# Where GpSimd waits for the two output DMAs in the closing barrier of a one-token decode kernel

## The chip, the cores and the metric

The kernel runs on one core of one Trainium2 chip. The metric is device time in microseconds (us) of one execution, read over several executions. The profile's *span* runs from the first to the last recorded instruction; in the profiled executions of before the time is 1.79 us more than the span (383.49 against 381.698). All times inside a profile count from the start of the span.

Engines: PE is TensorE, DVE is VectorE, ACT is ScalarE, POOL is GpSimd, SP is SyncE. A name with a small q (POOLq) is that engine's sequencer, under which the profile lists waits, drains and semaphore instructions.

## The reference

It is one decode step, with one token: grouped-query attention over a cache of 65,536 keys with 32 query heads and 4 key/value heads, plus a gated MLP branch, mixed by a sigmoid gate. Cut to what matters:

```python
x = A_x                                             # (1, 1, 1024) bf16
g = sigmoid((x * gate_w).sum(-1, keepdims=True))
a = A_ref(x, k_cache, v_cache, wq, wo)              # k_cache, v_cache: (1, 4, 65536, 128) bf16
b = B_ref(x, w_in, w_sp, b_sp, w_out)
return g * a + (1 - g) * b                          # (1, 1, 1024) bf16
```

Nearly all of the work is reading the two caches and the weights. The result is 2 KB.

## The kernel before

The body loads 162 MB through one ring of buffers, computes along, and ends with the output projection, a cast on ACT and two output DMAs of 1 KB. One is issued by ACT, one by SP:

```python
out_sb = const.tile([P, NO], BF16, name="out_sb")
out_rows = out.rearrange("o t (q n) -> (o t q) n", n=NO)
nc.scalar.copy(out=out_sb[:], in_=out_ps[:])
for i, queue in enumerate((nc.scalar, nc.sync)):
    p0 = (2 * i + 1) * B - 1
    ins = queue.dma_start(out=out_rows[2 * i:2 * i + 2, :], in_=out_sb[p0:p0 + 2, :])
    out_queues.append(ins.ins.name)
```

After the body stands a closing block. Its job is to make sure that every engine and every DMA is done, to reset the semaphores, and to let all engines go. This kernel already rewrites that block into one barrier, in which GpSimd is the hub. The framework gives GpSimd eight instructions there: `l[0]` drain, `l[1]` gather, `l[2]` (dropped), `l[3]` drain, `l[4]` range clear of the semaphores, `l[5]` drain, `l[6]` (dropped), `l[7]` release. The waits for all DMAs and engines, which the framework gives to SP, are hung on `l[0]`:

```python
def close_with_one_barrier(n):
    block = n.main_func.blocks[-1]
    # ... (collects each engine's instructions of the block as l = [(index, kind, ins), ...])
        if engine == mybir.EngineType.Pool:
            # ... (asserts the eight kinds)
            drop += [l[2][0], l[6][0]]
            closer = l[0][0]
            continue
        # ... (SP: takes over the waits; other engines: drop the second barrier)
    final = set()                       # the semaphores of the two output DMAs
    for b in n.main_func.blocks:
        for ins in b.instructions:
            if ins.name in out_queues:
                final |= {u.id for u in ins.sync_info.on_update}
    assert len(final) == len(out_queues)
    waits.sort(key=lambda w: w.id in final)
    block.instructions[closer] = copy.replace(
        block.instructions[closer], sync_info=mybir.SyncInfo(on_wait=waits, on_update=[]))
    for i in sorted(drop, reverse=True):
        del block.instructions[i]
```

There are eleven waits. The build puts wait instructions of two semaphores each in front of it and leaves the last wait on the drain. The semaphores that matter here: S[102] is the ACT output DMA, S[103] the SP output DMA, S[96] the gather (each other engine adds one with its closing drain; in the trace of before S[96] changes 0.001 to 0.013 us after the end of each of these four drains), S[97] the release, S[99] GpSimd's own work. S[105] and S[107] are DVE's and ACT's work.

Of the kernel before, what the change touches and what calls it, by code (L numbers as in the profile page):

```python
# [28 lines left out]
def kernel(  # L29
# [89 lines left out]
    def close_with_one_barrier(n):  # L119
        block = n.main_func.blocks[-1]  # L120
        by = {}
        for i, ins in enumerate(block.instructions):
            by.setdefault(ins.engine, []).append((i, type(ins).__name__, ins))
        drop = []
        waits = None
        for engine, l in by.items():
            kinds = [k for _, k, _ in l]
            if engine == mybir.EngineType.Pool:
                assert kinds == ["InstDrain", "InstEventSemaphore", "InstEventSemaphore",
                                 "InstDrain", "InstISA", "InstDrain", "InstEventSemaphore",  # L130
                                 "InstEventSemaphore"]
                drop += [l[2][0], l[6][0]]
                closer = l[0][0]
                continue
            if engine == mybir.EngineType.SP:
                assert l[0][2].has_wait() and not l[0][2].has_update()
                waits = list(l[0][2].sync_info.on_wait)
                drop.append(l[0][0])
                l, kinds = l[1:], kinds[1:]
            assert kinds == ["InstDrain", "InstEventSemaphore"] * 2  # L140
            drop += [l[1][0], l[2][0]]
        final = set()
        for b in n.main_func.blocks:
            for ins in b.instructions:
                if ins.name in out_queues:
                    final |= {u.id for u in ins.sync_info.on_update}
        assert len(final) == len(out_queues)
        waits.sort(key=lambda w: w.id in final)
        block.instructions[closer] = copy.replace(
            block.instructions[closer], sync_info=mybir.SyncInfo(on_wait=waits, on_update=[]))  # L150
        for i in sorted(drop, reverse=True):
            del block.instructions[i]

    nc.at_finalize(close_with_one_barrier)

    kv = big.tile([P, NKV * CT * P], BF16, name="kv")
# [405 lines left out]
```

## Time and profile before

| | before |
|---|---|
| median of 3 runs | 383.50 us (383.31 to 383.65) |
| span of the profiled run | 381.698 us |
| DMA engines busy | 9 tenths in 39 of 40 slices, 425 GB/s mean |
| two output DMAs issued | 379.721 us (SP), 379.725 us (ACT) |
| their semaphores complete | 380.853 us (ACT), 381.028 us (SP) |
| last arrival to the end of the span | 0.670 us |

The page of the kernel before: total span, the DMA rows of its 40 equal slices, and the chain of work that ended last, by engine and then by line:

```profile
span 381.7 us, 2586 instructions
...
DMA  9999999999999999999999999999999999999995
GB/s 376 438 419 422 433 435 440 433 471 415 407 426 440 440 441 426 440 433 440 440 428 440 440 440 433 434 427 426 412 433 441 433 440 413 428 419 433 433 414 220
...
## 4 chain that ended last, share of the span: by engine, by line
DMA 60%; PE 20%; DVE 15%; issue 1%; ACT 1%; SPq 1%; DVEq 0%; ACTq 0%
```

The chain in order of time has as its last long piece the load of A_wo (start in us, length in us, what):

```profile
347.56 31.38 DMA kv<-in_A_wo_dram
```

The kernel is bound by its loads, and this one ends at 378.94 us. A change to its last 2 us can't move the total by more than half a per cent. Here is the end of the timeline of the kernel before (start in us, length in us, engine, line, operation, operands, and in brackets the idle time before it and what ended it):

```profile
378.98 0.29 PE L475 MATMUL out_ps<-kv,oa 128*32 128x256 bf16 x4 [0.36 <-DMA kv<-in_A_wo_dram]
379.32 0.37 ACT L518 CAST out_sb<-out_ps 128x256 bf16<-128x256 f32 x1 [45.57 <-PE out_ps L475]
379.72 0.32 SPq L521 DMA_DIRECT2D out_dram<-out_sb  x1
379.73 0.25 ACTq L521 DMA_DIRECT2D out_dram<-out_sb  x1
```

After 379.73 us no engine computes any more. What fills the rest are sequencer instructions, which the timeline leaves out, but the view of one source line shows them. All of the close has one line (L557, the end of the kernel's context). Below are its instructions that ran between the issue of the output DMAs and the last arrival at 381.03 us (engine, operation, count, shortest/median/longest duration in ns, first and last start in us):

```profile
L557 ACTq DRAIN  x1: 241/241/241, 380.0 to 380.0; - x1
L557 SPq DRAIN  x1: 177/177/177, 380.1 to 380.1; - x1
L557 POOLq EVENT_SEMAPHORE  x1: 43/43/43, 380.9 to 380.9; - x1
```

And the same view after the last arrival, 381.03 to 381.7 us:

```profile
L557 POOLq EVENT_SEMAPHORE  x3: 17/17/42, 381.1 to 381.6; - x3
L557 POOLq DRAIN  x3: 34/41/72, 381.1 to 381.5; - x3
L557 POOLq EVENT_SEMAPHORE_RANGE_CLEAR  x1: 96/96/96, 381.4 to 381.4; - x1
```

So before the arrival GpSimd does one wait, and after it seven instructions. The exact order is in the single records of the trace. The table gives for each of GpSimd's instructions its start, the start counted from the last arrival, and the *step*, which is the distance to the start of the next one:

```
kernel before        start us   from arrival   step us
wait S[102],S[105]    380.877      -0.151       0.175
   (S[103] complete at 381.028: the last arrival)
wait S[103],S[107]    381.052      +0.024       0.087
drain (waits S[99])   381.139      +0.111       0.085
gather (S[96])        381.224      +0.196       0.080
drain                 381.304      +0.276       0.101
range clear           381.405      +0.377       0.125
drain                 381.530      +0.502       0.064
release (S[97])       381.594      +0.566
end of span           381.698      +0.670
```

The engines had all reported to S[96] by 380.272 us, so the gather had nothing to wait for at 381.224. It only stood behind an instruction that did. The reset and the release show in the trace too: S[99] to S[110] change 0.021 to 0.069 us after the range clear starts, and the other engines' last instructions start 0.041 to 0.053 us after the release does.

### The profile page before, as it was taken

To read this page: it belongs to the slowest core of one execution; us is meant where nothing else is said; L and a number is where in the kernel's file an instruction comes from. 1 tells how busy PE (TensorE), PEld (TensorE's weight loads), DVE (VectorE), ACT (ScalarE), POOL (GpSimd) and SP (SyncE) were. 2 spreads that over 40 slices of the span, in tenths; PEclk is the share of its full clock that TensorE was granted. 3 is DMA by queue.
4 is the path that set the end of the run, shared out by engine and by line. 5 is a ranking of instruction groups with operands and counts; after the bars stand their busy time and mean duration, and the time that the engine had idled before them with its cause. 6 is when DMAs were issued, how large, how long until landed. Compare 5 with 4: busy or idle time off the path is not lost.

```text
span 381.7 us, 2586 instructions
## 1 busy us (share of the span) xinstructions
PE 229.4 (60%) x1372; PEld 56.6 (15%) x796; DVE 218.4 (57%) x211; ACT 39.6 (10%) x55; POOL 4.4 (1%) x10
## 2 busy tenths in 40 slices
PE   0433465678157934796379539762977196749355
PEld 0110011112011200121011101110111011212123
DVE  4241487996689306966996058669860497550040
ACT  1010001111601100114011001140100010500000
POOL 4000000000000000000000000000000000000000
PEclk9996569998669885989598958995889599969768
DMA  9999999999999999999999999999999999999995
GB/s 376 438 419 422 433 435 440 433 471 415 407 426 440 440 441 426 440 433 440 440 428 440 440 440 433 434 427 426 412 433 441 433 440 413 428 419 433 433 414 220
DMA packets 4376, 162.17 MB, mean 425 GB/s; under 512 B 521, under 2 KB 525, under 8 KB 909
## 3 DMA queue, kind: packets, MB, share of 16 engines
q1 hardware_dynamic: 4324, 162.01, 98.7%
q8 instruction: 8, 0.13, 0.1%
q14 instruction: 4, 0.02, 0.0%
q10 hardware_dynamic: 40, 0.01, 0.0%
HBM read 162.01 MB, written 0.00 MB: 424 GB/s over the span
## 4 chain that ended last, share of the span: by engine, by line
DMA 60%; PE 20%; DVE 15%; issue 1%; ACT 1%; SPq 1%; DVEq 0%; ACTq 0%
DMA kv<-in_A_k_cache_dram 38%; PE s_ps L388 15%; DVE kv L381 9%; DMA kv<-in_A_wo_dram 8%; DMA kv<-in_A_wq_dram 7%; DMA kv<-in_A_v_cache_dram 7%; PE o_ps L434 3%; DVE pt L424 2%; DVE mx L383 1%; DVE o_sb L448 1%; PE q_ps L274 1%; ACT sc L421 1%; DVE rowt L444 1%; ACT sc L399 1%; SPq L165 1%
## 5 line engine op out<-in xcount | busy, mean ns | idle before, releaser
L388 PE MATMUL s_ps<-kv,wt 128*128 128x512 bf16 x512 | 138.1, 427 | 85.4 <-DVE kv L381 85.4
L381 DVE STREAM_TRANSPOSE kv<-kv 128x2048 int32<-128x2048 int32 x64 | 142.7, 2280 | 58.8 <-DMA kv<-in_A_k_cache_dram 58.8
L434 PE MATMUL o_ps<-kv,pt 128*64 128x512 bf16 x512 | 62.6, 404 | 7.5 <-DMA kv<-in_A_v_cache_dram 7.5
L388 PEld LDWEIGHTS <-wt 128*128 128x128 bf16 x256 | 27.1, 106 | 197.7 <-issue 133.8
L399 ACT CAST sc<-s_ps 128x1024 bf16<-128x1024 f32 x16 | 16.2, 1013 | 253.0 <-PE s_ps L388 253.0
L434 PEld LDWEIGHTS <-pt 128*64 128x64 bf16 x256 | 16.2, 116 | 51.3 <-issue 48.4
L424 DVE STREAM_TRANSPOSE pt<-sc 128x1024 bf16<-128x1024 bf16 x16 | 18.6, 1217 | 6.8 <-ACT sc L421 6.8
L444 DVE TENSOR_TENSOR rowt<-o_ps,own 128x1024 f32<-128x1024 f32 x4 | 4.8, 1195 | 25.7 <-PE o_ps L434 25.7
L421 ACT ACTIVATE sc<-sc,nb 128x1024 bf16<-128x1024 bf16 x16 | 18.2, 1137 | 12.2 <-DVE nb L417 12.2
L383 DVE TENSOR_REDUCE mx<-sc 128x1 f32<-128x1024 bf16 x12 | 14.5, 1206 | 7.0 <-ACT sc L399 7.0
L454 PE MATMUL om_ps<-o_sb,hsel 128*32 128x128 f32 x8 | 2.5, 421 | 19.7 <-DVE o_sb L448 19.7
L403 DVE TENSOR_REDUCE mx<-sc 128x1 f32<-128x1024 bf16 x4 | 4.9, 1220 | 13.6 <-ACT sc L399 13.6
L274 PE MATMUL q_ps<-kv,xT 128*32 128x512 bf16 x64 | 7.2, 630 | 7.3 <-DMA kv<-in_A_wq_dram 7.3
L274 PE MATMUL z_ps<-kv,xT 128*32 128x448 bf16 x64 | 6.4, 577 | 3.9 <-DMA kv<-in_B_w_in_dram 3.9
L475 PE MATMUL out_ps<-kv,oa 128*32 128x256 bf16 x128 | 6.5, 364 | 3.3 <-DMA kv<-in_A_wo_dram 1.9
L341 DVE TENSOR_TENSOR rowt<-q_ps,own_b 128x512 f32<-128x512 f32 x2 | 1.3, 686 | 12.4 <-PE q_ps L274 12.4
L448 DVE TENSOR_REDUCE o_sb<-rowt 128x128 f32<-128x1024 f32 x4 | 7.5, 1872 | 0.1
L289 DVE TENSOR_TENSOR rowt<-z_ps,own_b 128x448 f32<-128x448 f32 x2 | 1.2, 620 | 8.6 <-PE z_ps L274 8.6
L274 PEld LDWEIGHTS <-xT 128*32 128x32 bf16 x64 | 3.0, 139 | 19.3 <-issue 19.3
L230 PE MATMUL xb_ps<-xg,spread 8*128 8x256 bf16 x1 | 0.4, 367 | 9.0 <-DMA xg<-in_gate_w_dram 9.0
L475 PEld LDWEIGHTS <-oa 128*32 128x32 bf16 x128 | 4.5, 129 | 5.5 <-issue 2.7
L518 ACT CAST out_sb<-out_ps 128x256 bf16<-128x256 f32 x1 | 0.4, 372 | 45.6 <-PE out_ps L475 45.6
(88 smaller groups left out, 54.9 us busy)
## 6 DMA issues: line engine op xcount, KB each, us to landing
kv<-in_A_k_cache_dram SPq DMA_DIRECT2D x4, 4096.0 KB, 26.8
kv<-in_A_wq_dram SPq DMA_DIRECT2D x2, 4096.0 KB, 32.9
kv<-in_A_v_cache_dram SPq DMA_DIRECT2D x2, 4096.0 KB
kv<-in_B_w_in_dram SPq DMA_DIRECT2D x2, 3584.0 KB, 15.1
kv<-in_A_wo_dram SPq DMA_DIRECT2D x1, 4096.0 KB
kv<-in_B_w_out_dram SPq DMA_DIRECT2D x1, 3584.0 KB
kv<-in_A_wo_dram SPq DMA_DIRECT2D x1, 2048.0 KB, 28.1
kv<-in_A_wo_dram SPq DMA_DIRECT2D x1, 1024.0 KB, 30.2
```

Source lines behind the costliest of these rows:

```text
L274: ins = nc.tensor.matmul(ps[t * B:(t + 1) * B, k * HN:k * HN + n], lhsT=xT[:, i * KH + c:i * KH + c + 1].to_broadcast([P, B]), rhs=w[:, c, ...
L381: nc.vector.transpose(out=kb[:, v * n:(v + 1) * n], in_=kb[:, v * n:(v + 1) * n])
L383: nc.vector.reduce_max(**late.pop())
L388: ins = nc.tensor.matmul(s_ps[:, k * HN:(k + 1) * HN], lhsT=wt[g % 2][:, v, b].rearrange("p a v h -> p (a v h)"), rhs=kx[:, b // 2, b % 2, ...
L399: nc.scalar.copy(out=sct[g, j][:], in_=s_ps[:])
L403: nc.vector.reduce_max(**late.pop())
L421: nc.scalar.activation(out=sct[g, j][:], in_=sct[g, j][:], func=ACT.Exp, scale=SCALE, bias=nb[:, 0:1], accum_out=lss[g][:, j:j + 1])
L424: nc.vector.transpose(out=ptt[g, j][:].rearrange("p c x -> p (c x)"), in_=sct[g, j][:])
L434: ins = nc.tensor.matmul(o_ps[g][hs, e, :], lhsT=ptt[g, j][:, 2 * u:2 * u + 2, :].rearrange("p c x -> p (c x)"), rhs=vx[:, 2 * u + e], sta ...
L444: nc.vector.tensor_tensor(out=om8, in0=o_ps[g][:].rearrange("p e (v d) -> p (e v) d", d=DH), in1=own_8[:].unsqueeze(2).to_broadcast([P, 2 ...
L448: nc.vector.tensor_reduce(out=o_sb[:], in_=om8.rearrange("p x d -> p d x"), axis=AX.X, op=ALU.add)
L475: nc.tensor.matmul(out_ps[t * B:(t + 1) * B, :], lhsT=vec[:, c0 + c:c0 + c + 1].to_broadcast([P, B]), rhs=w[:, c, t * NO:(t + 1) * NO], st ...
```

## The change

The intent is to let GpSimd do its first drain and the gather while the output DMAs are still on their way, and to wait for these two DMAs only at the second drain, just before the semaphores are reset. That they must have arrived by then is my argument. What the trace of before shows is that the reset reaches their semaphores: S[102] and S[103] change once more 0.025 and 0.043 us after the range clear starts, when both DMAs are complete since 380.853 and 381.028 us. The diff:

```diff
-                closer = l[0][0]
+                closer, reset = l[0][0], l[3][0]
+                assert not l[3][2].has_wait() and not l[3][2].has_update()
                 continue
...
-        waits.sort(key=lambda w: w.id in final)
-        block.instructions[closer] = copy.replace(
-            block.instructions[closer], sync_info=mybir.SyncInfo(on_wait=waits, on_update=[]))
+        for at, w in ((closer, [w for w in waits if w.id not in final]),
+                      (reset, [w for w in waits if w.id in final])):
+            block.instructions[at] = copy.replace(
+                block.instructions[at], sync_info=mybir.SyncInfo(on_wait=w, on_update=[]))
```

The built program shows what becomes of it. GpSimd gets four waits of two semaphores, the drain, the gather, then a wait for S[103] alone, the second drain with S[102] as its wait, the clear, the third drain and the release. No instruction is added and none is removed.

## The prediction

> **What bounds the kernel now.** The page's 40 slices show the DMA engines at 9 tenths in every slice but the last, 425 GB/s mean, 162 MB in a span of 381.7 us. The chain that ended last is 60% DMA; its last long piece is the A_wo load, 31.38 us from 347.56 us. The change touches none of this. After that load come the last projection matmuls, the ACT cast at 379.32 us and the two output DMAs issued at 379.72 us (timeline). From there on only the close runs, about 2.0 us, 0.5% of the span: the ceiling on everything here.
>
> **The close, from the trace's single records of the closing line L557.** The ACT output DMA's semaphore is complete at 380.853 us, the SP one's at 381.028 us. ACT and SP start their closing drains at 380.019 and 380.094 us; all engines have reported to the barrier by 380.272 us. GpSimd starts its last DMA wait at 381.052 us, its drain at 381.139, the gather of the other engines at 381.224, a second drain at 381.304, the semaphore range clear at 381.405, a third drain at 381.530, the release at 381.594; the span ends at 381.698. So 0.67 us follow the last arrival, all serial, mostly on GpSimd's sequencer. The gather waits for nothing there.
>
> **What the change does.** By the order of the built programs, the first waits keep the load semaphores, DVE, ACT and GpSimd's own; then come drain and gather; then a wait for the SP output semaphore alone, the second drain with the ACT output semaphore as its wait, then the clear. GpSimd still has five wait instructions, four in front and one behind. Other engines are unchanged. First drain and gather move from behind the last arrival into the 0.75 us of idle time before it. They cost 0.085 us (drain to gather) and 0.080 us (gather to drain), start to start.
>
> **How much is on the critical path.** All of the 0.165 us, since nothing else follows the last arrival. A wait of one semaphore may be slightly shorter: steps of 0.080 us after the one-semaphore gather, 0.087 us after the two-semaphore wait. The second drain now carries a wait; the first one, which did, took 41 ns against the plain one's 72, so it should cost no more. Estimated saving 0.16 to 0.19 us, 0.04 to 0.05%. The output DMAs' 1.1 to 1.3 us from issue to arrival stay exposed. [...] so I count start-to-start spacing: the trace agrees, with 41 ns of drain in an 85 ns step.
>
> **Prediction.** 383.5 - 0.17 = 383.3 us, 8 in 10 between 382.9 and 383.7 (the three runs before span 0.34 us, twice the gain). Faster by over 2%: 0.005; within 2%: 0.99; slower by over 2%: 0.005.
>
> **What the profile would show.** Right: gather started near 380.3 to 380.4 us, before the output arrivals; last wait within 0.03 us of the last arrival; range clear about 0.19 us after it instead of 0.377; span end about 0.5 us after it instead of 0.67. Wrong: a drain with a wait taking over 0.1 us, a gather still late, or the arrivals themselves moved by more than the gain.
>
> **What would make it wrong.** Output DMA latency that varies by tenths of a us between executions, or spread in the 380 us of loads before it; either can hide or double the gain without being its doing.

The forecast's sum: 0.085 + 0.080 = 0.165 us of steps and up to 0.087 - 0.080 = 0.007 us for the wait, put at 0.17 us together, and 383.5 - 0.17 = 383.3 us.

## The result

| | before | after |
|---|---|---|
| median, same rounds (5 runs each) | 383.62 us (383.31 to 383.75) | 383.38 us (383.30 to 383.59) |
| last arrival | 381.028 us | 381.028 us |
| from there to the range clear | 0.377 us | 0.186 us |
| from there to the end of the span | 0.670 us | 0.480 us |

The ratio of the times is 0.9997 with a 95% interval of 0.9983 to 1.0011. (A ratio here is the one for the fast runs; it is close to, but not exactly, the ratio of the medians, 0.9994, or of the means, 0.9996.) By the clock on the wall the verdict is thus "the same": 0.19 us would be 0.05%, and the interval is wider than that. In the trace, however, the gain can be read to a few ns, since by chance the last arrival fell on the same 381.028 us in both profiled runs.

The page after, the rows that answer to those of before:

```profile
span 381.5 us, 2586 instructions
...
DMA  9999999999999999999999999999999999999995
...
## 4 chain that ended last, share of the span: by engine, by line
DMA 60%; PE 19%; DVE 17%; issue 2%; ACT 1%; SPq 1%; DVEq 0%; ACTq 0%
```

The last long piece of its chain in order of time:

```profile
346.49 32.36 DMA kv<-in_A_wo_dram
```

The chain is the same to a per cent or two: the loads still bound the kernel. The last load ends at 378.85 us, 0.09 us earlier than before, but that lead is gone by the cast. The end of the timeline after:

```profile
378.89 0.40 PE L477 MATMUL out_ps<-kv,oa 128*32 128x256 bf16 x4 [0.25 <-DMA kv<-in_A_wo_dram]
379.34 0.37 ACT L520 CAST out_sb<-out_ps 128x256 bf16<-128x256 f32 x1 [44.91 <-PE out_ps L477]
379.74 0.32 SPq L523 DMA_DIRECT2D out_dram<-out_sb  x1
379.75 0.25 ACTq L523 DMA_DIRECT2D out_dram<-out_sb  x1
```

The output DMAs were issued even 0.02 us later than before, so the shorter span doesn't come from earlier loads. The closing line (now L559) from the issue to the last arrival, 379.7 to 381.03 us:

```profile
L559 POOLq EVENT_SEMAPHORE  x2: 17/334/651, 379.1 to 380.3; - x2
L559 POOLq DRAIN  x1: 41/41/41, 379.8 to 379.8; - x1
L559 ACTq DRAIN  x1: 240/240/240, 380.0 to 380.0; - x1
L559 SPq DRAIN  x1: 171/171/171, 380.1 to 380.1; - x1
```

And after the last arrival, 381.03 to 381.6 us:

```profile
L559 POOLq EVENT_SEMAPHORE  x2: 17/17/17, 381.1 to 381.4; - x2
L559 POOLq DRAIN  x2: 34/53/72, 381.1 to 381.3; - x2
L559 POOLq EVENT_SEMAPHORE_RANGE_CLEAR  x1: 96/96/96, 381.2 to 381.2; - x1
```

(The record of 651 ns is an earlier wait, of S[110] and S[107], which starts at 379.1 us and ends just after ACT's cast.) The drain of 41 ns and the gather of 17 ns now stand before the arrival (379.8 and 380.3 us), and only five GpSimd instructions are left after it instead of seven. In single records:

```
kernel after         start us   from arrival   step us
drain (waits S[99])   379.797      -1.231       0.518
gather (S[96])        380.315      -0.713       0.737
   (S[103] complete at 381.028: the last arrival)
wait S[103]           381.052      +0.024       0.061
drain (waits S[102])  381.113      +0.085       0.101
range clear           381.214      +0.186       0.125
drain                 381.339      +0.311       0.063
release (S[97])       381.402      +0.374
end of span           381.508      +0.480
```

Before, 0.353 us lie between the first wait behind the arrival and the clear: 0.087 + 0.085 + 0.080 + 0.101. After, 0.162 us: 0.061 + 0.101. The difference of 0.191 us consists of the two steps that moved away (0.085 + 0.080 = 0.165 us) and of the wait, which now holds one semaphore instead of two (0.087 - 0.061 = 0.026 us; what makes a wait shorter is taken up under "Both output semaphores in one wait").

### The profile page after: what moved, and what is told of

Same layout as the page of the kernel before. It is cut to its first block, busy times and chain, and to the rows that moved or that the text cites. A ratio compares the mean times of both kernels' runs of the same rounds, so it can differ in the third digit from the quotient of the medians.

```text
span 381.5 us, 2586 instructions
## 1 busy us (share of the span) xinstructions
PE 229.9 (60%) x1372; PEld 56.5 (15%) x796; DVE 218.4 (57%) x211; ACT 39.6 (10%) x55; POOL 4.4 (1%) x10
## 4 chain that ended last, share of the span: by engine, by line
DMA 60%; PE 19%; DVE 17%; issue 2%; ACT 1%; SPq 1%; DVEq 0%; ACTq 0%
DMA kv<-in_A_k_cache_dram 37%; PE s_ps L390 14%; DVE kv L383 10%; DMA kv<-in_A_wo_dram 8%; DMA kv<-in_A_wq_dram 7%; DMA kv<-in_A_v_cache_dram 7%; PE o_ps L436 3%; DVE pt L426 2%; DVE mx L385 2%; DVE o_sb L450 1%; PE q_ps L276 1%; ACT sc L423 1%; DVE rowt L446 1%; ACT sc L401 1%; SPq L167 1%
## 5 line engine op out<-in xcount | busy, mean ns | idle before, releaser
L390 PE MATMUL s_ps<-kv,wt 128*128 128x512 bf16 x512 | 140.5, 433 | 84.1 <-DVE kv L383 84.1
L436 PE MATMUL o_ps<-kv,pt 128*64 128x512 bf16 x512 | 60.7, 394 | 7.7 <-DMA kv<-in_A_v_cache_dram 7.7
```

Of the source, the lines that this page charges most:

```text
L390: ins = nc.tensor.matmul(s_ps[:, k * HN:(k + 1) * HN], lhsT=wt[g % 2][:, v, b].rearrange("p a v h -> p (a v h)"), rhs=kx[:, b // 2, b % 2, ...
L436: ins = nc.tensor.matmul(o_ps[g][hs, e, :], lhsT=ptt[g, j][:, 2 * u:2 * u + 2, :].rearrange("p c x -> p (c x)"), rhs=vx[:, 2 * u + e], sta ...
```

## The experiments

Three theories were put to the test.

- *Serial tail.* After the last output arrival GpSimd's sequencer alone decides when the kernel ends. Each instruction behind the arrival costs its start-to-start step, and each one in front of it is free as long as it fits. The whole gain is then the steps that moved, plus the shorter wait.
- *Drift.* The 0.19 us between the two profiles is chance, for instance in when the loads or the output DMAs ended.
- *Shape of the waits.* Most of the gain comes from how the waits are packed (one or two semaphores, on a drain or alone), not from what was moved.

In all of them the stretch "last arrival to range clear" is the measure, and "last arrival to end of span" beside it. Unlike the total time it doesn't contain the 380 us of loads, which vary by tenths of a us: in the profiles, save one slow one, the last arrival fell anywhere from 380.909 to 381.256 us. All kernels gave the correct result, and every time is set against runs of the kernel before on the same chip.

| kernel | arrival to clear, us | arrival to end of span, us | mean time less that of before, us (runs) |
|---|---|---|---|
| before | 0.377 | 0.670 | |
| after | 0.186 | 0.480 | -0.16 (5 to 5) |
| after, again | 0.185 | 0.478 | -0.13 (5 to 9) |
| gather first | 0.279 | 0.572 | -0.14 (1 to 9) |
| late pair | 0.195 | 0.488 | -0.18 (1 to 9) |
| waits swapped | 0.125 | 0.418 | -0.38 (1 to 1) |
| both on the clear | 0.085 | 0.377 | -0.26 (1 to 1) |
| split waits | 0.024 | 0.317 | -0.27 (5 to 9) |
| split waits, again | 0.025 | 0.318 | -0.37 (5 to 9) |
| before + 12 drains | 1.106 | 1.400 | +0.74 (4 to 7) |
| after + 12 drains | 0.185 | 0.478 | -0.25 (4 to 7) |
| before + 40 drains | 2.816 | 3.114 | +2.79 (3 to 7) |
| after + 40 drains | 1.539 | 1.831 | +1.53 (4 to 7) |

(For "before + 40 drains" the trace columns are of its second profile and the time is of the three fast runs. Where a kernel ran once, its time decides nothing here, and only its trace is used.)

### The change once more

No edit.

> The changed kernel once more, with more rounds. Serial-tail theory (only instructions that stand behind the last output arrival count, each with its start-to-start step): from the last arrival to the range clear 0.186 us again (0.377 before), to the span's end 0.48 us, and a mean time 0.1 to 0.3 us below before, likely not resolved. Drift theory (the 0.19 us between the two profiles is chance): the stretch from the last arrival to the range clear differs from the first profile by 0.05 us or more.

Measured: 0.185 us to the clear, 0.478 us to the end, each step behind the arrival within 1 ns of the first profile, although the last arrival came 0.009 us earlier. The mean time was 383.28 us against 383.41 us; the ratio is 0.9997 (0.9983 to 1.0010). The tail repeats to 2 ns, so drift can't explain it. The total time stays unresolved.

### Half of the change: only the gather moves

```diff
 # kernel before, at the end of close_with_one_barrier
+        pool = [i for i, x in enumerate(block.instructions)
+                if x.engine == mybir.EngineType.Pool]
+        g = block.instructions[pool[1]]          # the gather
+        del block.instructions[pool[1]]
+        block.instructions.insert(pool[0], g)    # in front of all waits and the first drain
```

> Half of the change: the gather stands first of all GpSimd closing instructions, but all waits stay together in front of the first drain, as before. Serial tail: arrival, two-semaphore wait, drain, drain, clear: the range clear starts 0.29 to 0.30 us after the last arrival (0.377 before, 0.186 in the change). If the gather alone were worth the gain: 0.19 to 0.21. If nothing of it: 0.37.

Measured: 0.279 us, so a saving of 0.098 us, about half, and 0.011 us better than the lower end of what was expected. The steps tell why: with the gather gone, the first drain is followed by a drain, and that step is 0.068 us, whereas drain to gather took 0.085 us. The removed time is 0.085 + 0.080 - 0.068 = 0.097 us. A step here thus belongs to a pair of neighbours, not to one instruction. The gain divides between gather and drain much as the serial tail says.

This run is also a warning about spans. Its span, 381.481 us, is shorter than that of the full change (381.508), though its close is 0.092 us longer, because its last arrival came at 380.909 us.

### Both output semaphores in one wait

Here both output semaphores are hung on the gather instruction. The build makes of it an early wait for S[96] and then one instruction that waits for S[102] and S[103] and also resets S[96].

```diff
-                closer, reset = l[0][0], l[3][0]
+                closer, reset = l[0][0], l[1][0]        # l[1] is the gather
...
+            old = block.instructions[at].sync_info
             block.instructions[at] = copy.replace(
-                block.instructions[at], sync_info=mybir.SyncInfo(on_wait=w, on_update=[]))
+                block.instructions[at], sync_info=mybir.SyncInfo(
+                    on_wait=w + list(old.on_wait if at == reset else []),
+                    on_update=list(old.on_update if at == reset else [])))
```

> Drain and the wait for the other engines early, as in the change, but both output semaphores are waited for by one instruction of two semaphores, which also resets the gather. Tells the cost of a two-semaphore wait from the rest. Serial tail with steps of 0.087 us (two semaphores) and 0.061 us (one): range clear 0.21 us after the last arrival, 0.026 more than the change. If the number of semaphores of a wait is worth nothing: 0.186. If it is the main part of the gain: above 0.28.

Measured: 0.195 us, 0.009 us more than the change instead of 0.026. The record of the pair starts at 380.770 us, 0.024 us after S[102] was complete, and the drain behind it starts 0.094 us after S[103]. In the kernel before, the pair was the other way round: S[103], the late one, stood first and S[107], long complete, second. The late pair also resets a semaphore, which the other does not, so these two alone can't tell the order from the reset. The traces hold a pair that can. In the changed kernel S[110],S[107] stands in front of the first drain, waits for its second semaphore and resets nothing: the drain starts 0.074 us after S[107]. In the kernel before, the same drain starts 0.111 us after S[103], the first of its pair. (S[107] is an engine's semaphore and not a DMA's, but the pair S[109],S[101] of the kernel before, whose second belongs to a load and comes last, takes 0.074 us too.) So which semaphore of the pair comes last is worth 0.037 us here. The late pair, which also resets a semaphore, takes 0.020 us more, 0.094 against 0.074; that the reset is what costs it is an estimate from this difference, since a plain drain follows it and not the drain that waits for S[99]. Behind a wait for S[103] alone the drain starts 0.085 us after the arrival, between the two pairs: in these traces the number of semaphores by itself doesn't set the cost. What is shown for the gain is that the packing of the waits is worth 0.009 to 0.026 us here, not the main part of 0.19, so the third theory falls as the main cause. My number for this run was too high because I took the step of one pair for that of any pair.

### The same cost, amplified: 12 and 40 more drains

The difference of 0.19 us is too small for the clock on the wall. So GpSimd got more of what the change moves: plain drains between the first drain and the gather, in both kernels at the same place.

```diff
+        pad = [copy.replace(block.instructions[closer], name=f"I-{900000 + i}",
+                            sync_info=mybir.SyncInfo(on_wait=[], on_update=[]))
+               for i in range(12)]                      # or 40
         for i in sorted(drop, reverse=True):
             del block.instructions[i]
+        at = next(i for i, x in enumerate(block.instructions)
+                  if x.engine == mybir.EngineType.Pool) + 1
+        for x in reversed(pad):
+            block.instructions.insert(at, x)
```

> As with 40 drains, with 12: serial tail: time 0.8 to 1.2 us above before, 384.4 to 384.8 us.

> The same 12 drains in the changed kernel, where they fit or nearly fit into the idle time before the last arrival. Serial tail: last arrival to range clear as in the change without them (0.186 us, at most 0.1 more), time as before or 0.2 us below, 383.3 to 383.6 us, and 0.9 to 1.3 us below the kernel before with the same 12 drains, which 3 rounds resolve. If the early place is not free: within 0.3 us of the padded kernel before.

The closing line of the kernel before with 12 drains, after its last arrival at 381.256 us:

```profile
L564 POOLq DRAIN  x15: 34/34/72, 381.4 to 382.5; - x15
L564 POOLq EVENT_SEMAPHORE  x3: 17/17/43, 381.3 to 382.6; - x3
L564 POOLq EVENT_SEMAPHORE_RANGE_CLEAR  x1: 96/96/96, 382.4 to 382.4; - x1
```

The changed kernel with the same 12 drains, before its last arrival at 380.936 us:

```profile
L566 POOLq DRAIN  x13: 34/34/41, 379.7 to 380.4; - x13
L566 POOLq EVENT_SEMAPHORE  x2: 17/278/540, 379.1 to 380.5; - x2
```

All 12 stand behind the arrival in the one and before it in the other. One plain drain after another takes a step of 0.061 us, of which the record shows 34 ns. The tail grew to 1.400 us in the kernel before and stayed at 0.478 us in the changed one. The times follow: 384.05 to 384.48 us against 383.11 to 383.34 us, with means that differ by 0.99 us where the traces say 0.92, within the 0.9 to 1.3 us expected. No run of the one comes near a run of the other; the two 95% intervals against before still overlap (1.0001 to 1.0034, and 0.9979 to 1.0009). Each of the two times was missed, though: the kernel before lost 0.74 us instead of 0.8 to 1.2, since a plain drain's step is less than I had put it at, and the changed one ran at 383.24 us in the mean, below 383.3 to 383.6.

> The kernel before with 40 more GpSimd drains between its first drain and the gather. Serial tail: all 40 steps are exposed; at 0.065 to 0.1 us each (estimate from the steps of 0.063 to 0.101 us after plain drains) span and time grow by 2.6 to 4.0 us, so about 386 to 387.5 us, and the time grows by what the trace shows between last arrival and gather. Rival (the runtime hides GpSimd's closing work from the timed span): time unchanged though the trace shows the steps.

> The same 40 drains at the same place in the changed kernel, where they start when ACT's cast is done (first drain at about 379.8 us), not after the last arrival. Serial tail: about 1.15 us of them fit into the time until the last arrival at 381.03 us, so the loss is 1.1 to 1.5 us smaller than in the kernel before with the same drains: 1.4 to 2.9 us above before. Drift or no slack: the same loss as in the padded kernel before, apart from 0.19 us.

Forty drains are more than the idle time holds. The traces give tails of 3.11 and 1.83 us, a difference of 1.28 us, and the times differ by 1.26 us (386.28 and 385.02 us, means of the fast runs). The intervals against before are clear of each other: 1.0056 to 1.0090 and 1.0025 to 1.0055. In the changed kernel 21 of the 43 drains started before the arrival, from 379.8 us on:

```profile
L566 POOLq DRAIN  x21: 34/34/46, 379.8 to 381.0; - x21
```

So the room in front of the arrival is about 1.24 us for a drain (379.794 to 381.036 us), over seven times the 0.165 us that the change moves into it. My estimate for the drains was a bit high: 2.6 us at least, against 2.44 us in the trace. That the time grew by 2.79 us, inside the range, is luck: it comes from an extra 0.35 us that I had not foreseen.

Two things in these runs were not expected. First, that extra: both kernels padded with 40 drains lost about 0.35 us more in time than in span: time less span was 2.13 to 2.15 us in the profiled runs instead of 1.8 us. With 12 drains it stayed at 1.8 us. It is the same in both kernels, so their difference isn't touched; its cause stays open. Second, the profile of the padded kernel before fell in an execution of 570.75 us. Its matmuls took 827 ns instead of 427, as its groups of instructions show:

```profile
L395 PE MATMUL s_ps<-kv,wt 128*128 128x512 bf16 x512 | 305.3, 827 | 22.4 <-DVE kv L388 12.7 <-issue 9.8
```

That execution is left out of every comparison of times, and what caused it stays open: its trace holds no record of the granted clock (the view of its cores prints 1.000, which is also what it prints without any record; the three fast runs have 0.843 to 0.860), so it can't show whether the clock had a part in it. The kernel was run again for a profile of its own:

> The kernel before with 40 more late drains again, because its first profile fell in an execution of 570.75 us in which all matmuls took twice as long. Serial tail: last arrival to range clear 2.815 us and to the span's end 3.11 us, as in that profile, since the close does not depend on the state of the loads before it; time 386.2 to 386.4 us.

Measured: 2.816 us to the clear and 3.114 us to the end (2.815 and 3.109 in the slow execution), time 386.42 us, 0.02 us above the range. Even an execution of 570 us has the same close to 5 ns.

### How far can the waits move?

In both profiles S[103] came 0.175 us after S[102], and in the changed kernel it is the earlier of the two waits that has to wait for it. Three variants place the waits differently. The first only swaps the two:

```diff
-                      (reset, [w for w in waits if w.id in final])):
+                      (reset, sorted((w for w in waits if w.id in final), key=lambda w: -w.id))):
```

> The change with its two last waits swapped: first a wait for ACT's output semaphore alone, then the second drain waits for SP's, which arrived 0.175 us later in both profiles. Serial tail: only the drain stands behind the last arrival: range clear 0.12 to 0.13 us after it (0.186 in the change). If a wait at a drain is served more slowly than at a plain wait: 0.18 or more. If SP's semaphore is not the later one every time, no gain in this execution.

Measured: 0.125 us. The wait on the drain was served as fast as the one by itself: 0.025 us after the arrival, against 0.024 in the changed kernel. The second hangs both on the range clear, behind the second drain:

```diff
-                closer, reset = l[0][0], l[3][0]
-                assert not l[3][2].has_wait() and not l[3][2].has_update()
+                closer, reset = l[0][0], l[4][0]          # l[4] is the range clear
+                assert not l[4][2].has_wait() and not l[4][2].has_update()
```

> Both output semaphores after the second drain: a wait for SP's alone, then the clear waits for ACT's. Serial tail: wait step 0.061 us plus 0.024: range clear 0.085 us after the last arrival, span end about 0.38 us after it. If the clear needs its drain directly in front: wrong output, or a step above 0.1 us between wait and clear.

Measured: 0.085 us and a correct output. The third puts ACT's semaphore on the second drain and SP's, the later one, on the clear. This saves the separate wait instruction:

```diff
+        early, late = [], []
+        # ... (late: the semaphore of SP's output DMA; early: that of ACT's)
         for at, w in ((closer, [w for w in waits if w.id not in final]),
-                      (reset, [w for w in waits if w.id in final])):
+                      (reset, [w for w in waits if w.id in early]),
+                      (clear, [w for w in waits if w.id in late])):      # clear = l[4][0]
```

> ACT's output semaphore is waited for at the second drain, SP's (the later by 0.175 us) at the range clear itself. Serial tail: the second drain too goes before the last arrival; range clear 0.02 to 0.03 us after the arrival, span end 0.31 to 0.34 us after it, against 0.48 for the change; time 0.35 us below before, about 383.2. Rival (a clear that carries a wait is dearer, or the clear needs the drain just in front): the step from arrival to clear stays above 0.1 us or the output is wrong.

Measured: the clear starts 0.024 us after the last arrival and the span ends 0.317 us after it. The means are 383.14 us against 383.41 us, ratio 0.9993 (0.9980 to 1.0006). It was run again:

> The split waits once more, for the repeat of the time on other executions. Serial tail: last arrival to range clear 0.024 us and to the span's end 0.317 us; mean time 0.2 to 0.4 us below before. If the 0.27 us of the first five runs was chance: within 0.1 us of before.

Measured: 0.025 and 0.318 us; 383.16 us against 383.53 us, ratio 0.9991 (0.9977 to 1.0004). In both calls all five runs of the split waits lie below all nine of before (382.95 to 383.29 against 383.32 to 383.48 us, then 383.02 to 383.31 against 383.42 to 383.67 us), though both intervals still hold 1. The closing line of this second run after its last arrival at 381.012 us:

```profile
L565 POOLq EVENT_SEMAPHORE_RANGE_CLEAR  x1: 96/96/96, 381.0 to 381.0; - x1
L565 POOLq DRAIN  x1: 34/34/34, 381.2 to 381.2; - x1
L565 POOLq EVENT_SEMAPHORE  x1: 17/17/17, 381.2 to 381.2; - x1
```

Only the clear, the drain behind it and the release are left of GpSimd's close. In the traces this version beats both kernels, by 0.353 us the one before and by 0.163 us the changed one. A clear in front of the arrival was not tried: that it has to stay behind is my argument, which no run shows. Whether the drain behind the clear is needed was not tried either.

## Why the prediction was right

- *What bounds the kernel, and the ceiling.* Right. The loads fill the span in both profiles (DMA engines at 9 tenths in 39 of 40 slices), and the edit changed no instruction outside GpSimd's close.
- *What moves.* Right. The drain and the gather ran at 379.797 and 380.315 us, before the arrivals. The prediction had said 380.3 to 380.4 us for the gather.
- *All of it on the critical path.* Right, and shown from three sides. The tail shrank by the steps that were taken out, in the full change and in half of it. 12 drains in the early place left the tail at 0.478 us; in the old place they lengthened it by 0.73 us and the time by 0.74 us. Time and trace agree on the differences (0.99 against 0.92 us with 12 drains, 1.26 against 1.28 us with 40).
- *The size.* The prediction said 0.17 us, 0.16 to 0.19. The trace shows 0.190 us to the end of the span, the upper edge. The moved steps were right to the ns (0.165 us). The term that was mis-sized is "a wait of one semaphore may be slightly shorter": it was put at 0.080 us, after the gather, which also waits for one semaphore but resets it as well. A wait alone took 0.061 us. That is 0.019 us, the difference between 0.172 and 0.191, and close to the 0.020 us that the late pair, which also resets a semaphore, took more.
- *The second drain with a wait costs no more.* Right: 72 ns and a step of 0.101 us with and without it.
- *Counting steps, not durations.* The prediction took this from the trace, with 41 ns of drain in a step of 85 ns. The runs bear it out: by durations the drain and the gather moved are 41 + 17 = 58 ns, while the tail lost 165 ns by them. One wait does lie inside a record: the late pair's record starts 0.024 us after its first semaphore and is 181 ns long, so it holds the wait for the second.
- *The time.* 383.38 us was measured for 383.3 us predicted. The chances given (0.99 for within 2%) fit. The times alone wouldn't have confirmed the gain, as the prediction said of itself: its range of 382.9 to 383.7 us also holds the 383.62 us of the kernel before, so that the time fell into it says nothing of the mechanism. What was feared, output DMAs that vary by tenths of a us, did not occur: SP's took 1.29 to 1.31 us from issue to complete semaphore in all 14 profiles. The last arrival's spread comes from before the issue, which fell anywhere from 379.603 to 379.946 us outside the slow execution.

Left on the table was that the same argument applies to the second drain, and to which of the two output semaphores is waited for last. The prediction stopped at what the change did.

## What to carry to other kernels

In a closing barrier like this one, hang each wait on the last instruction that needs it. What stands in front then ran in the shadow of the output DMAs here: the drain and the gather, 0.165 us of steps, fitted into the 1.231 us between the start of this drain and the arrival. And let the latest arrival be awaited by the instruction that needs it, not by a separate wait before it: with SP's wait on the clear itself the clear started 0.024 us after the arrival, with a separate wait in front 0.085 us after it. To judge a gain of 0.05%, measure in the trace from the event that the gain follows (here the last arrival) instead of comparing times. And if the clock on the wall is to confirm it, multiply the suspected cost in both places until the difference stands out.

## Figures of the closing instructions and the output DMAs

- Start-to-start steps on GpSimd: plain drain to plain drain 0.061 us (34 ns reported), a wait of one semaphore 0.061 us, or 0.080 us in front of a drain if it also resets it, of two 0.087 us when both are there by the time its record starts, drain to range clear 0.101 us, clear to drain 0.125 us. From the last semaphore of a wait to the start of the next instruction: 0.085 us (one semaphore), 0.111 us (two, the first comes last), 0.074 us (two, the second comes last).
- The record of a wait for two semaphores starts before both are there when the second comes last: the late pair's record starts 0.024 us after the first one and holds the wait for the second (181 ns), as does the record of 651 ns in the changed kernel. The pair S[109],S[101] of the kernel before shows the same: its record starts 0.024 us after S[109] and is 2.600 us long, until 0.030 us after S[101].
- The closing drains are 34 to 72 ns long on GpSimd, 164 to 180 ns on SP and 240 to 246 ns on ACT in the profiles quoted here.
- The output DMAs of 1 KB took 1.11 to 1.13 us (ACT) and 1.29 to 1.31 us (SP) from issue to complete semaphore, in 14 profiles.
- In the kernel before S[102] changes at 380.154 us and then twice more, at 380.823 and 380.853 us, for a DMA of two rows. SP's DMA, issued 4 to 5 ns before ACT's, completed 0.174 to 0.175 us after it in every profile. The cause stays open.
- Both kernels with 40 more drains had 2.13 to 2.15 us of time beyond the profiled span, against 1.8 us: about 0.35 us more, whose cause stays open.
